# Retention and top-1 mixture of experts on one core: weight transfers moved behind GpSimd's scalings, their waits taken out

## The chip, the cores and the metric

The kernel runs on one core of one Trainium2 chip. The metric is the device time of one execution in microseconds (us), the median of several runs. The engines are named as in the profile: PE (TensorE, its weight loads apart as PEld), DVE (VectorE), ACT (ScalarE), POOL (GpSimd) and SP (SyncE, which here only issues DMAs).

## The reference

Eight heads of a decaying, causal linear attention over 8 sequences of 576 tokens, and behind it a top-1 mixture of 8 experts over all 4608 tokens. Cut to what matters:

```python
scores = (q @ k.T) / sqrt(64)                     # q, k, v: (8, 8, 576, 64)
D = where(i >= j, gamma[h] ** (i - j), 0)         # gamma = 1 - 2 ** (-5 - h)
x = ((scores * D) @ v), heads side by side        # (4608, 512)
logits = x @ w_gate                               # (4608, 8)
e = argmax(logits, axis=1)
gate = softmax(logits)[e]
out[token] = gate * (relu(x @ w1[e]) @ w2[e])     # w1: (8, 512, 1024), w2: (8, 1024, 512)
```

## The kernel before

The program has two phases. Phase 1 (the loop at L693) computes x, writes it as bf16 rows to the DRAM tensor x_rows, and routes the tokens of the first half. Phase 2 (L807 to L849) runs the experts: it gathers the rows of an expert, transposes them (trans), multiplies by w1 (mm1, PSUM tile pm), by w2 (mm2, PSUM tile py), and scatters the result.

Phase 1 goes over 40 blocks, i = 0 to 39: five for each sequence b, numbered c = 0 to 4. Blocks with c = 0 to 3 hold 128 tokens, the block with c = 4 the last 64. The five blocks of a sequence are called a batch here. The decay is split into a factor for each row of k and one for each row of q, so that k and q are scaled on POOL before PE sees them:

- scale_q(b, p) (L241) writes qq, one of two buffers; scale_k(i) (L250) writes kk, one of three. Both run on POOL. A block of the loop scales q for the next sequence, scale_q(b + 1, c), and k three blocks ahead, scale_k(i + 3).
- stage_TK(i + 2) transposes kk on PE into the PSUM tile psk, and ACT copies it to kT. stage_TQ(b + 1, c) transposes the qq that the same block has just scaled (psq). So PE wants qq in the block in which POOL makes it, and kk one block later.
- stage_R(i - 1) transposes the finished x back (psr) and writes it through SP's queue. For c = 4 its source is xTr. stage_L1 and stage_L2 make the logits (psl).
- stage_S(i + 1) updates the state from kk and v (pss); stage_AV(i) and stage_IN(i) add the two parts of the output in PSUM (psx), which DVE copies to xT; stage_SC(i + 1) makes the scores (pssc), which DVE multiplies by the mask into sc. `mark` keeps the last sc, kT, xT and se instruction.

The order on each engine is the order in which the program is written (a manual schedule). Around the change it is, in each block: scale_q, scale_k, load_k(i + 6), TK, TQ, L2, R, L1, S, AV, IN, SC, load_v(i + 6), then the weight transfers, then a step of the routing generator `rf` (L655, on DVE and PE, and one expert's two gathers xg on POOL per step once the slots are known).

The weights of experts 0 to 3 are fetched during phase 1 by load_w (L224), a DMA that POOL issues and that turns float32 in DRAM into bf16 in SBUF: 8 parts an expert, each 256 KB of bf16. Which block issues which part is a table (L688): one part each behind blocks 12, 16, 20, 24 and 28, three parts each behind blocks 33 to 39, and the last six behind the loop. Before, each of them waits: the first of a block for sc of block i + 1, the second for kT of block i + 2, the third for xT of block i:

```python
for (e, j), m in zip(early.get(i, ()), ("sc", "kT", "xT")):
    load_w(e, j, 4, wpool, mark.get(m))
```

POOL takes its instructions in order, so what stands behind a waiting transfer waits with it: scale_q and scale_k of the next block.

Of the kernel before, what the change touches and what calls it, by code (L numbers as in the profile page):

```python
# [41 lines left out]
def kernel(  # L42
# [22 lines left out]
    def after(ins, dep):  # L65

        if dep is not None:
            tc.add_manual_dep(ins.ins, dep.ins.name,
                              mybir.DependencyInfo(mybir.DependencyClass.Sync, mybir.DependencyReason.DATA),
                              reason="pace")  # L70
# [6 lines left out]
    wpool = ctx.enter_context(tc.tile_pool(name="wts", bufs=4))  # L77
# [20 lines left out]
    def load_q(b, g, dep=None, eng=None):  # L98

        if g == 0:  # L100
            qts[b] = ldq.tile([P, H, NCH, DH], F32, tag="q", name="qt")
        hs = slice(g * NP, (g + 1) * NP)
        after((eng or nc.sync).dma_start(out=qts[b][:, hs, :, :],
                                         in_=q[b, hs, 0:NCH * P, :].rearrange("h (p s) d -> p h s d", p=P)), dep)

    def load_kv(store, tag, src, i, dep):
        b, c = blocks[i]
        store[i] = ldk.tile([P, H, DH], F32, tag=tag, name=tag + "t")
        after(nc.sync.dma_start(out=store[i][:, :, :],
                                in_=src[b, :, c * P:(c + 1) * P, :].rearrange("h p d -> p h d")), dep)  # L110

    def load_k(i, dep=None):

        if i >= NB:
            return
        b, c = blocks[i]
        if c < NCH:
            load_kv(kts, "k", k, i, dep)
            return
        kts[i] = ldk.tile([P, H, DH], F32, tag="k", name="kt")  # L120
        for u in range(2):
            after(nc.sync.dma_start(out=kts[i][u * REM:(u + 1) * REM, :, :],
                                    in_=(q, k)[u][b, :, NCH * P:S, :].rearrange("h p d -> p h d")), dep)
# [100 lines left out]
    def load_w(e, part, n, pool, dep=None):  # L224

        if part == 0:
            wb[e] = (pool.tile([P, NPT, F], BF16, tag="w1", name="w1b"),
                     pool.tile([P, NFB, DM], BF16, tag="w2", name="w2b"))
        m = (NPT, NFB)[part // n] // n
        o = part % n * m  # L230
        w = (moe_w1, moe_w2)[part // n]
        after(nc.gpsimd.dma_start(out=wb[e][part // n][:, o:o + m, :],  # L232
                                  in_=w[e, o * P:(o + m) * P, :].rearrange("(c p) f -> p c f", p=P)), dep)
# [5 lines left out]
    mark = {}  # L239

    def scale_q(b, p):  # L241
        h0 = 2 * p
        qq = wkp.tile([P, NCH, P], F32, tag="qq")
        nc.gpsimd.tensor_tensor(  # L244
            out=qq[:, :, :].rearrange("p s (h d) -> p h s d", d=DH), in0=qts[b][:, h0:h0 + 2, :, :],
            in1=qg[:, 0:NCH, h0:h0 + 2].rearrange("p s h -> p h s").unsqueeze(3)
                .to_broadcast([P, 2, NCH, DH]), op=ALU.mult)
        qqs[(b, p)] = qq

    def scale_k(i):  # L250
        if i >= NB:
            return
        kk = wk3.tile([P, H, DH], F32, tag="kk")
        nc.gpsimd.tensor_tensor(out=kk[:, :, :], in0=kts.pop(i)[:, :, :],  # L254
                                in1=kg[:, blocks[i][1], :].unsqueeze(2).to_broadcast([P, H, DH]), op=ALU.mult)
        kks[i] = kk

    def stage_TQ(b, p):

        qq = qqs.pop((b, p))  # L260
        pst = psw.tile([P, 512], F32, tag="W", name="psq")
        for s_ in range(NCH):
            tr(pst[:, s_:512:NCH], qq[:, s_, :], ident[:, :])
        if b not in qTs:
            qTs[b] = wkp.tile([P, NP, 512], F32, tag="qT", name="qT")
        nc.scalar.copy(out=qTs[b][:, p, :], in_=pst[:, :])

    def stage_TK(i):
        if i >= NB:
            return  # L270
        kk = kks[i]
        pst = psw.tile([P, 512], F32, tag="W", name="psk")
        for p in range(NP):
            tr(pst[:, p * P:(p + 1) * P], kk[:, 2 * p:2 * p + 2, :].rearrange("p h d -> p (h d)"), ident[:, :])
        kT = wkp.tile([P, NP, P], F32, tag="kT")
        mark["kT"] = nc.scalar.copy(out=kT[:, :, :].rearrange("p a t -> p (a t)"), in_=pst[:, :])  # L276
        kTs[i] = kT
# [130 lines left out]
    def stage_L1(b):  # L408

        ps = psw.tile([P, 512], F32, tag="W", name="psl")  # L410
        xT, xTr = xTs.pop(b), xTs.pop((b, "r"))
        for a in range(NP):
            for c in range(NCH):
                mm(ps[32 * c:32 * c + 32, 0:P], wgp[:, 0, a, :], xT[:, c, a * P:(a + 1) * P], a == 0, a == NP - 1)
        for p in range(NP):
            o = (2 * (p % 2) + p // 2) * DH
            mm(ps[32 * p:32 * p + 32, P:P + DH], wgp[:, 1, p, :], xTr[:, o:o + DH], True, True)
        lt = wk1.tile([P, P + DH], F32, tag="lt")
        nc.vector.tensor_copy(out=lt[:, :], in_=ps[:, 0:P + DH])
        lts[b] = lt  # L420

    def stage_L2(b):
        lt = lts.pop(b)
        ps2 = psw.tile([P, 512], F32, tag="W", name="psl2")
        tr(ps2[:, 0:P], lt[:, 0:P], ident[:, :])
        tr(ps2[0:DH, P:2 * P], lt[:, P:P + DH], ident[:, :])
        t0 = b * NCOL
        nc.vector.tensor_copy(out=lg[:, t0:t0 + NCH, :],
                              in_=ps2[:, 0:P].rearrange("p (c n) -> p c n", n=32)[:, :, 0:E])
        nc.vector.tensor_reduce(out=lg[0:DH, t0 + NCH, :],  # L430
                                in_=ps2[0:DH, P:2 * P].rearrange("p (c n) -> p n c", n=32)[:, 0:E, :],
                                axis=AX.X, op=ALU.add)
# [18 lines left out]
    def make_routing():  # L451

        nc.gpsimd.memset(lg[:, :, :], 0.0)
        nc.gpsimd.memset(su1[:, :], -1.0)
        nc.gpsimd.affine_select(out=su1[:, :], in_=su1[:, :], pattern=[[-1, P]], base=0, channel_multiplier=1,
                                compare_op=ALU.is_ge, fill=0.0)
        nc.gpsimd.memset(onesb[:, :], 1.0)
        nc.gpsimd.tensor_copy(out=identb[:, :], in_=ident[:, :])
        nc.gpsimd.iota(iota_r[:, :], pattern=[[1, P]], base=0, channel_multiplier=0,
                       allow_small_or_imprecise_dtypes=True)  # L460
        nc.gpsimd.iota(rev[:, :], pattern=[[-1, E]], base=E, channel_multiplier=0,
                       allow_small_or_imprecise_dtypes=True)
        nc.gpsimd.memset(off[:, :], 0.0)
        nc.gpsimd.memset(off[REM:P, :].rearrange("p (b c) -> p b c", c=NCOL)[:, :, NCH:NCOL], 100.0)
        nc.gpsimd.memset(rst[:, :, :], 1.0)
        nc.gpsimd.memset(rst[:, :, 0:1], 0.0)
        nc.gpsimd.iota(hi[:, :], pattern=[[S // 64, B], [2, NCOL]], base=0, channel_multiplier=0,
                       allow_small_or_imprecise_dtypes=True)
        nc.gpsimd.iota(lo[:, :], pattern=[[1, 1]], base=1, channel_multiplier=1,
                       allow_small_or_imprecise_dtypes=True)  # L470
        nc.gpsimd.tensor_copy(out=fld[:, :, 0], in_=hi[:, :])
        nc.gpsimd.tensor_copy(out=fld[:, :, 1], in_=lo[:, :].to_broadcast([P, NT]))
# [215 lines left out]
    early = {12 + 4 * j: [(0, j)] for j in range(5)}  # L688
# [4 lines left out]
    for i, (b, c) in enumerate(blocks):  # L693
        if i == 1:
            make_routing()

        if c < NP and b + 1 < B:
            scale_q(b + 1, c)
        scale_k(i + 3)
        load_k(i + 6, mark.get("sc"))  # L700
        stage_TK(i + 2)
        if c < NP and b + 1 < B:
            stage_TQ(b + 1, c)
        if c == 1 and b > 0:
            stage_L2(b - 1)
        if i > 0:
            stage_R(i - 1)
        if c in (1, 3) and b + 2 < B:
            load_q(b + 2, c // 2, mark.get("kT"))
        if c == 0 and b > 0:  # L710
            stage_L1(b - 1)
        stage_S(i + 1)
        stage_AV(i)
        stage_IN(i)
        stage_SC(i + 1)
        load_v(i + 6, mark.get("xT"))
        for (e, j), m in zip(early.get(i, ()), ("sc", "kT", "xT")):
            load_w(e, j, 4, wpool, mark.get(m))
        if (b, c) == (B // 2, 1):
            rf = route_first()  # L720
        if rf is not None:
            steps(rf, 1.4)
# [232 lines left out]
```

## Time and profile before

| | us |
|---|---|
| median of 3 runs | 406.07 |
| lowest and highest run | 403.64, 408.64 |
| the profiled execution | 403.17 |
| its span, first to last instruction | 401.4 |

The profile shows one execution; its rows are times from the start of its span. Some 1.8 us lie outside the span. PE was busy for 338.4 us of it, POOL for 196.9, DVE for 161.1 and ACT for 127.4. The mean granted clock of TensorE was 0.95 of full speed.

### The profile page before, as it was taken

The numbers are of one execution on the slowest core, as the hardware profiler recorded it, in microseconds if no ns is written. First come the engines' busy times: TensorE is split into PE (matmuls) and PEld (weight loads), VectorE is DVE, ScalarE is ACT, GpSimd is POOL, SyncE is SP. The second block draws the span as 40 slices with busy tenths as digits, with TensorE's granted clock in tenths as the row PEclk, the third lists the DMA queues.
The fourth block names the chain that finished last, engine by engine and source line by source line (L and its number), as shares of the span: only waits on it lengthen the run. The fifth ranks groups of instructions, "written<-read, shape, count | busy, mean of one in ns | idle before, by whom it ended". The sixth has DMA issues, their size and how long they took to land.

```text
span 401.4 us, 11092 instructions
## 1 busy us (share of the span) xinstructions
PE 338.4 (84%) x4642; PEld 248.8 (62%) x4642; DVE 161.1 (40%) x358; ACT 127.4 (32%) x292; POOL 196.9 (49%) x241
## 2 busy tenths in 40 slices
PE   2599998889797969899668499989999999999950
PEld 2478787677676758678556367745555656566520
DVE  2043444315243627874165778323322322222220
ACT  2233434323331513423222022332233233342400
POOL 4784434161616153441875535785656555555120
PEclk9999999989998969999898679999999999999995
DMA  8969888766686766775999999989978332323120
GB/s 213 244 108 226 198 215 191 194 155 168 152 201 153 190 129 163 181 167 135 174 184 167 207 207 212 241 156 265 198 173 159 135 104 91 119 94 104 61 72 6
DMA packets 113084, 65.35 MB, mean 163 GB/s; under 512 B 83838, under 2 KB 105342, under 8 KB 113024
## 3 DMA queue, kind: packets, MB, share of 16 engines
q0 software_dynamic: 18176, 31.47, 35.9%
q1 hardware_dynamic: 93792, 32.02, 34.0%
q10 hardware_dynamic: 1056, 1.05, 0.9%
q8 instruction: 39, 0.64, 0.7%
q14 instruction: 21, 0.17, 0.1%
HBM read 67.14 MB, written 15.20 MB: 205 GB/s over the span
## 4 chain that ended last, share of the span: by engine, by line
PE 49%; issue 4%; DVE 3%; POOL 3%; DMA 1%; ACT 1%; SPq 0%; POOLq 0%; DVEq 0%; ACTq 0%
PE pm L60 18%; PE py L60 17%; PE psx L60 4%; PE pt L63 2%; PE pssc L60 2%; DMA x_rows<-xr 1%; PE psr L63 1%; POOL xg L637 1%; PE pss L60 1%; DVE xt L764 1%; PE psk L63 1%; PE psl L60 1%; PE pspl L60 1%; PE psq L63 1%; POOL kk L254 1%
## 5 line engine op out<-in xcount | busy, mean ns | idle before, releaser
L780 ACT ACTIVATE ht<-pm 128x384 bf16<-128x384 f32 (+1 forms) x96 | 50.6, 527 | 101.3 <-PE pm L60 100.8
L60 PE MATMUL pm<-xt,w1b 128*128 128x256 bf16 (+1 forms) x512 | 75.0, 307 | 2.4 <-DVE xt L764 2.4
L60 PE MATMUL py<-w2b,ht 128*128 128x512 bf16 x320 | 71.7, 379 | 0.0
L254 POOL TENSOR_TENSOR kk<-kt,kg 128x512 f32<-128x512 f32 x40 | 41.8, 1048 | 57.6 <-PE pss L60 25.3
L795 POOL DMA_INDIRECT out_dram<-ys,tids x40 | 40.9, 1022 | 59.4 <-DVE ys L794 52.7
L60 PEld LDWEIGHTS <-w1b 128*128 128x128 bf16 x512 | 51.3, 100 | 25.6 <-DVE xt L764 2.2
L60 PEld LDWEIGHTS <-ht 128*128 128x128 bf16 x320 | 30.8, 98 | 34.1
L794 DVE TENSOR_SCALAR ys<-py,gat 128x512 f32<-128x512 f32 x40 | 30.0, 750 | 47.5 <-PE py L60 44.9
L356 DVE COPY xT<-psx 128x512 f32<-128x512 f32 x32 | 22.1, 692 | 65.4 <-PE psx L60 65.4
L276 ACT COPY kT<-psk 128x512 f32<-128x512 f32 x40 | 23.8, 594 | 77.0 <-PE psk L63 50.5
L637 POOL DMA_INDIRECT xg<-x_rows,tidg x40 | 41.5, 1037 | 12.2 <-issue 7.9
L311 DVE TENSOR_TENSOR sc<-pssc,mask 128x1024 f32<-128x1024 f32 x32 | 39.1, 1222 | 19.6 <-issue 13.6
L63 PE MATMUL psk<-ident,kk 128*128 128x128 f32 x160 | 27.1, 293 | 18.2 <-POOL kk L254 18.2
L60 PE MATMUL psx<-sc,vt 128*64 128x128 f32 (+1 forms) x640 | 40.5, 278 | 0.8 <-DVE sc L311 0.8
L764 DVE COPY xt<-pt 128x512 bf16<-128x512 bf16 x40 | 15.5, 420 | 50.1 <-PE pt L63 47.3
L60 PE MATMUL pssc<-qT,kT 64*64 64x128 f32 (+1 forms) x1024 | 35.2, 257 | 0.0
L232 POOL DMA_DIRECT2D w1b<-in_moe_w_dram x24 | 15.4, 649 | 40.2 <-DVE sc L311 24.5
L244 POOL TENSOR_TENSOR qq<-qt,qg 128x512 f32<-128x512 f32 x32 | 33.9, 1061 | 1.8 <-DMA qt<-in_q_dram 1.4
L60 PEld LDWEIGHTS psx<-sc,vt 128*64 128x64 f32 (+1 forms) x640 | 32.7, 144 | 3.0 <-DVE sc L311 1.7
L63 PE MATMUL psq<-ident,qq 128*128 128x128 f32 x128 | 22.8, 309 | 13.6 <-POOL qq L244 13.6
L63 PEld LDWEIGHTS psk<-ident,kk 128*128 128x128 f32 x160 | 17.4, 144 | 24.1 <-POOL kk L254 20.0
L60 PEld LDWEIGHTS pssc<-qT,kT 64*64 64x64 f32 x1024 | 29.5, 137 | 1.8 <-issue 1.8
(118 smaller groups left out, 352.2 us busy)
## 6 DMA issues: line engine op xcount, KB each, us to landing
kt<-in_k_dram SPq DMA_DIRECT2D x32, 256.0 KB, 4.6
vt<-in_v_dram SPq DMA_DIRECT2D x32, 256.0 KB, 3.6
qt<-in_q_dram SPq DMA_DIRECT2D x14, 512.0 KB, 5.1
x_rows<-xr SPq DMA_DIRECT2D x32, 128.0 KB, 3.4
w1b<-in_moe_w_dram POOLq DMA_DIRECT2D x16, 256.0 KB, 6.3
w2b<-in_moe_w_dram POOLq DMA_DIRECT2D x16, 256.0 KB, 6.7
w1b<-in_moe_w_dram POOLq DMA_DIRECT2D x8, 512.0 KB, 7.2
w2b<-in_moe_w_dram POOLq DMA_DIRECT2D x8, 512.0 KB, 7.2
```

Source lines behind the costliest of these rows:

```text
L60: nc.tensor.matmul(out=out, lhsT=lhsT, rhs=rhs, start=start, stop=stop, skip_group_check=True)
L63: nc.tensor.transpose(out=out, in_=in_, identity=identity)
L244: nc.gpsimd.tensor_tensor(out=qq[:, :, :].rearrange("p s (h d) -> p h s d", d=DH), in0=qts[b][:, h0:h0 + 2, :, :], in1=qg[:, 0:NCH, h0:h0 ...
L254: nc.gpsimd.tensor_tensor(out=kk[:, :, :], in0=kts.pop(i)[:, :, :], in1=kg[:, blocks[i][1], :].unsqueeze(2).to_broadcast([P, H, DH]), op=A ...
L276: mark["kT"] = nc.scalar.copy(out=kT[:, :, :].rearrange("p a t -> p (a t)"), in_=pst[:, :])
L311: mark["sc"] = nc.vector.tensor_tensor(out=sc[:, :, :, :].rearrange("p j a i -> p j (a i)"), in0=pssc[:, :, :], in1=mask[:, :, :].rearrang ...
L356: mark["xT"] = nc.vector.tensor_copy(out=xTs[b][:, c, :].rearrange("p (w t) -> p w t", w=2), in_=psx[:, :, 0:2 * P])
L637: nc.gpsimd.indirect_dma_start(out=xg[:, :], out_offset=None, in_=x_rows[0:nr, :], in_offset=bass.IndirectOffsetOnAxis(ap=slots[ph][1][:, ...
L764: nc.vector.tensor_copy(out=xt[:, :, j * P:(j + 1) * P], in_=pt[:, :, :])
L780: nc.scalar.activation(out=ht[:, f0:f0 + per, :], in_=pm[:, :, :], func=AF.Relu)
L794: nc.vector.tensor_scalar(out=ys[:, :], in0=py[:, :], scalar1=gat[:, i:i + 1], scalar2=None, op0=ALU.mult)
L795: nc.gpsimd.indirect_dma_start(out=next(outs)[:, :], out_offset=bass.IndirectOffsetOnAxis(ap=tids[:, i:i + 1], axis=0), in_=ys[:, :], in_o ...
```

## The change

The weight transfers are issued right behind scale_k of their block, and they wait for no step of the block any more. The table of parts is the same.

```diff
@@ -697,6 +697,8 @@
         if c < NP and b + 1 < B:
             scale_q(b + 1, c)
         scale_k(i + 3)
+        for e, j in early.get(i, ()):
+            load_w(e, j, 4, wpool)
         load_k(i + 6, mark.get("sc"))
         stage_TK(i + 2)
         if c < NP and b + 1 < B:
@@ -714,8 +716,6 @@
         stage_IN(i)
         stage_SC(i + 1)
         load_v(i + 6, mark.get("xT"))
-        for (e, j), m in zip(early.get(i, ()), ("sc", "kT", "xT")):
-            load_w(e, j, 4, wpool, mark.get(m))
         if (b, c) == (B // 2, 1):
             rf = route_first()
         if rf is not None:
```

No engine's instructions change their order: between scale_k and the old place POOL has nothing else in a block. What changes is the waits. On POOL around block 12 (kk is the scaling of k for block 15, the row under w1b the scaling of q in block 13):

```order
 L254 TENSOR_TENSOR kk<-kt,kg 128x512 [waits DMAHW5_49,PE_49]
-L232 DMA w1b<-in_moe_w_dram 128x1024 [waits DVE_49]
+L232 DMA w1b<-in_moe_w_dram 128x1024
 L244 TENSOR_TENSOR qq<-qt,qg 128x2x4x64 [waits Pool_49]
 L254 TENSOR_TENSOR kk<-kt,kg 128x512 [waits DMAHW0_49,PE_49,Pool_49]
```

The transfer has lost its wait for DVE (sc of block 13); its place is the same. On POOL in blocks 33 and 34 (the first kk is that of block 36, the second that of block 37; xg are the gathers of expert 0, which need the slots tidg from DVE; DMASW0 to DMASW7 are eight completion counters that POOL's DMAs use in turn, each waiting for the one eight before it):

```order
 L254 TENSOR_TENSOR kk<-kt,kg 128x512 [waits DMAHW0_49,PE_49,Pool_49]
-L232 DMA w2b<-in_moe_w_dram 128x2x512 [waits DVE_49]
-L232 DMA w2b<-in_moe_w_dram 128x2x512 [waits Activation_49]
-L232 DMA w2b<-in_moe_w_dram 128x2x512
-L637 DMA xg<-x_rows,tidg_2892 128x512 [waits DMASW0_49]
+L232 DMA w2b<-in_moe_w_dram 128x2x512 x3
+L637 DMA xg<-x_rows,tidg_2892 128x512 [waits DMASW0_49,DVE_49]
 L637 DMA xg<-x_rows,tidg_2892 128x512 [waits DMASW1_49]
 L254 TENSOR_TENSOR kk<-kt,kg 128x512 [waits DMAHW4_49,PE_49]
```

Here the three transfers have lost their waits for DVE and ACT, and the first gather now names DVE itself. From block 34 on the transfers keep their wait for the counter of the eighth DMA before them.

## Rows read from the trace of the kernel before

**Rows 1.** The page, part 1: busy us (share of the span), instructions.

```profile
PE 338.4 (84%) x4642; PEld 248.8 (62%) x4642; DVE 161.1 (40%) x358; ACT 127.4 (32%) x292; POOL 196.9 (49%) x241
```

**Rows 2.** Who waited for whom: us in total, times, longest.

```profile
PE psq L63 <- POOL qq L244: 13.6, 6, 4.0
```

**Rows 3.** Timeline, PE, blocks 11 to 16: start, us, what, [idle before, releaser].

```profile
68.52 0.66 PE L63 MATMUL psk<-ident,kk 128*128 128x128 f32 x4
...
73.45 0.66 PE L63 MATMUL psk<-ident,kk 128*128 128x128 f32 x4
...
77.87 0.66 PE L63 MATMUL psk<-ident,kk 128*128 128x128 f32 x4
81.46 1.12 PE L63 MATMUL psq<-ident,qq 128*128 128x128 f32 x4 [2.94 <-POOL qq L244]
...
85.89 0.66 PE L63 MATMUL psk<-ident,kk 128*128 128x128 f32 x4
...
89.30 0.66 PE L63 MATMUL psk<-ident,kk 128*128 128x128 f32 x4
...
94.83 0.66 PE L63 MATMUL psk<-ident,kk 128*128 128x128 f32 x4
```

**Rows 4.** Timeline, POOL, the weight transfer of block 12; idle before and releaser.

```profile
79.55 0.76 POOL L232 DMA_DIRECT2D w1b<-in_moe_w_dram  x1 [7.24 <-DVE sc L311]
```

**Rows 5.** Timeline, PE, stage_R of c = 4, run in blocks 5, 10 and 30.

```profile
42.08 0.44 PE L63 MATMUL psr<-ident,xTr 128*128 128x128 f32 x2 [0.44 <-DVE xTr L379]
63.70 0.44 PE L63 MATMUL psr<-ident,xTr 128*128 128x128 f32 x2 [0.44 <-DVE xTr L379]
...
171.25 0.44 PE L63 MATMUL psr<-ident,xTr 128*128 128x128 f32 x2 [2.07 <-DVE xTr L379]
```

**Rows 6.** Timeline, PE, the first rows of blocks 34, 35 and 38.

```profile
188.62 0.66 PE L63 MATMUL psk<-ident,kk 128*128 128x128 f32 x4
...
195.92 0.66 PE L63 MATMUL psk<-ident,kk 128*128 128x128 f32 x4 [3.82 <-POOL kk L254]
...
215.15 0.66 PE L63 MATMUL psr<-ident,xT 128*128 128x128 f32 x4
```

**Rows 7.** Timeline, POOL, blocks 33 to 35: kk of blocks 36, 37 and 38.

```profile
180.98 1.04 POOL L254 TENSOR_TENSOR kk<-kt,kg 128x512 f32<-128x512 f32 x1 [0.92 <-POOL qq L244]
189.84 2.19 POOL L232 DMA_DIRECT2D w2b<-in_moe_w_dram  x3 [7.82 <-DVE sc L324]
...
194.81 1.05 POOL L254 TENSOR_TENSOR kk<-kt,kg 128x512 f32<-128x512 f32 x1
...
200.24 1.06 POOL L254 TENSOR_TENSOR kk<-kt,kg 128x512 f32<-128x512 f32 x1
```

**Rows 8.** Timeline, DVE: routing rows of block 29, and the slots of expert 0's gathers.

```profile
165.64 5.23 DVE L593 TENSOR_SCALAR rh<-iota_r,r 128x128 bf16<-128x128 bf16 x4
...
186.37 0.18 DVE L618 TENSOR_SCALAR tidg<-tid 128x16 int32<-128x16 f32 x1
```

**Rows 9.** The chain that ended last, in order of time: the last write of x_rows.

```profile
222.79 5.75 DMA x_rows<-xr
```

**Rows 10.** Timeline, DVE: the first copy of phase 2 and its wait.

```profile
228.66 0.76 DVE L764 COPY xt<-pt 128x512 bf16<-128x512 bf16 x2 [1.63 <-DMA x_rows<-xr]
```

**Rows 11.** Tile x_rows: landing of its transfers, all of them.

```profile
DMA to landing us min/median/max: 1.8/3.6/8.0
```

**Rows 12.** Busy us by window: PE, PEld, DVE, ACT, POOL, granted clock, DMA share, GB/s.

```profile
40.00:80.00 40.00, 36.89 (x772) 31.04 (x765) 16.89 (x24) 17.23 (x45) 14.23 (x15) 1.00 0.84 200
...
210.00:229.00 19.00, 12.08 (x226) 9.90 (x224) 11.53 (x38) 3.61 (x11) 11.78 (x18) 0.80 1.04 188
```

**Rows 13.** Timeline, POOL: transfers as phase 1 ends.

```profile
219.65 2.82 POOL L232 DMA_DIRECT2D w2b<-in_moe_w_dram  x4 [1.13 <-DVE sc L324]
...
229.52 0.70 POOL L232 DMA_DIRECT2D w2b<-in_moe_w_dram  x1 [0.69 <-DMA w2b<-in_moe_w_dram]
```

**Rows 14.** Tile kt: landing of its transfers, all of them.

```profile
DMA to landing us min/median/max: 2.9/4.4/8.1
```

## The prediction

> **What bounds the kernel now.** I read the busy times first, then the waits, then the timelines of PE and POOL in the stretches with weight transfers. PE is the busiest engine, 84% of the span, and POOL is half idle [rows 1]. So phase 1 should run at PE's speed unless something holds PE. In the list of waits PE's transposes of q wait 13.6 us in total for POOL's scaling [rows 2]. The timeline says when. The psk row marks the start of a block: blocks 11 and 12 take 4.93 and 4.42 us, block 14 takes 3.41 and block 15 5.53 [rows 3]. A whole undisturbed batch, blocks 5 to 10, takes 63.70 - 42.08 = 21.62 us [rows 5], which leaves 21.62 - 4.93 - 4.42 - 3.41 - 5.53 = 3.33 us for a block with c = 3. Block 13 has c = 3 and takes 8.02 us: PE waits 2.94 us for qq [rows 3]. The reader sees why on POOL: the transfer of block 12 waited 7.24 us for sc of block 13 [rows 4], and qq of block 13 stands behind it. [...]
>
> In block 33 it is the same with kk: kk of block 36 ends at 182.02, the three transfers start at 189.84, released by sc of block 34, and kk of block 37 follows at 194.81 [rows 7]. PE stands 3.82 us for it [rows 6].
>
> **The change, part by part.** No work is added or removed. At 26 transfers POOL no longer waits for DVE or ACT, and they keep their places in its order; what moves is the time at which POOL may go on.
>
> 1. *The five single transfers (blocks 12 to 28).* After the change the transfer of block 12 can start when kk before it ends, some 7 us earlier than 79.55, and qq of block 13 is done before PE asks for it, right behind the psk of 77.87 [rows 3]. From 63.70 to 171.25 four batches took 107.55 us, against 4 x 21.62 = 86.48 [rows 5]: an excess of 21.07 us. What of it stays? At 171.25 PE waits 2.07 us for xTr instead of the usual 0.44 [rows 5]; DVE stood in rows rh, four in 5.23 us [rows 8], while POOL caught up with the scalings that the transfer of block 28 had held back. Half of these 1.63 us I leave in, since some scalings will still fall there, and 0.6 us for the routing's matmuls and copies, which the undisturbed batch does not have (a choice; 0 and 2 are its bounds). 21.07 - 0.8 - 0.6 = 19.7 us won. The lower bound, if of each stall only the wait goes and the clock's part stays, is the 13.6 us of rows 2.
>
> 2. *Blocks 33 to 37.* From 188.62 to 215.15 PE needs 26.53 us for blocks 34 to 37 [rows 6]. Undisturbed they are 3.41, 5.53, 4.93 - 0.44 and 4.42 - 0.44 us, the 0.44 being four transposes of q that do not exist there (an estimate, two thirds of psk's 0.66, since neighbours overlap): 17.41. So 9.1 us are to be had, if kk comes in time. By POOL's order: the three transfers take 2.19 us [rows 7] and start at about 182.0; the two gathers wait for the slots, which DVE has at 186.6 [rows 8]; from the transfers' end to kk of block 37 the gathers took 194.81 - 192.03 = 2.8 us [rows 7]. So kk of block 37 starts at 189.4 and is there at 190.4; PE asks at 188.62 + 3.41 = 192.0. From one kk to the next, with three transfers and two gathers between, were 5.43 us [rows 7]: kk of block 38 is there at 195.9 (asked for at 197.6), that of block 39 at 201.3 (asked for at 202.1). The slack is 1.6, 1.7 and 0.8 us. I take the whole 9.1 us; zero is the lower bound.
>
> 3. *The end of phase 1.* The first expert's copies wait for the last x_rows write, which takes 5.75 us [rows 9] where the quickest takes 1.8 [rows 11]; the DMA engines are full there (share 1.04, [rows 12]). Will they still be? The transfers start 7.8 us earlier, but 27 of them at 1.4 us each (one of the last ones, 0.69 idle and 0.70 issuing, [rows 13]) are 38 us, and phase 1 ends 9 us earlier too. So the write meets the same crowd: 0 us. If the crowd were gone, the 1.63 us that DVE waited for it would be won and no more [rows 10]; if it were worse, 8.0 [rows 11] instead of 5.75 costs 2.3.
>
> 4. *The transfers' earlier place among k, v and q.* With PE undisturbed from 40 to 80 us the DMA share was 0.84 [rows 12]. One transfer in 21.6 us adds 1.4 us of full use, 0.065. That leaves about a tenth free; k takes 4.4 us to land, at most 8.1 [rows 14], and is wanted three blocks after its issue, 13 us. Cost 0. If the cover went, each of the four batches would be longer by up to the transfer's own 1.4 us: 0 to 5.6 in all.
>
> 5. *Phase 2.* Expert 0's eight parts land earlier than before. The last transfers stand at about the same place against the start of phase 2 as before (part 3), and they are expert 3's, which three others precede. 0.
>
> Sum: 19.7 + 9.1 = 28.8 us off the profiled execution's 403.17: 374.4. That execution is 2.9 us under the median of the runs, 406.07, and under the lowest of them; I put 2.1 us back and predict **376.5 us** as the median.
>
> [...] While POOL issued four transfers at 219.65 in 2.82 us [rows 13], 0.70 each, DVE was busy for 11.53 of the 19 us around [rows 12]; at 189.84, with DVE's sc behind them, three took 2.19, 0.73 each [rows 7]. But DVE's rh rows stood still beside POOL's scalings [rows 8]. [...]
>
> **Rivals.**
> [...]
> - *Only the waits go, the clock's part stays.* 13.6 instead of 19.7: 380.5, as a median 382.6. For: each gap need not vanish wholly. Against: in the 40 us up to the first transfer the granted clock was 1.00 [rows 12].
> - *Crowding, the slower side.* Without their waits the transfers compete with k and v. It decides once k lands later than 13 us after its issue. If each batch then were DMA-bound at 107.55 / 4 = 26.9 us, nothing is won in part 1, and in blocks 34 to 37 the nine transfers before kk of block 39 put 9 x 1.4 = 12.6 us ahead of the last k and v, with nothing won there either: 403.2 + 12.6 = 415.8. Against: 8.1 us is the longest landing of k [rows 14], and the last k is issued when only three transfers are ahead.
> - *It does nothing.* If other waits of the same rows (the counters, or POOL's own order) held the transfers as long, the time would be 406. For it speaks only that from block 34 on the counters stay.
>
> **How the numbers follow.** Forecast 0.72; lock or counters 0.11; clock's part stays 0.11; nothing 0.03; crowding 0.03. Low end: 374.4 less 1.6 for the last write and 1.4 for what part 1 left in, 371.4, so 371. High end: the two cases of partial gain are at 382.6 and 385.6, both together at 374.4 + 9.1 + 6.1 + 2.1 = 391.7; 389 leaves out the upper part of that and the last two cases. Faster by over 2% (what a measurement of this kernel can about tell from no change) 0.94, within 2% 0.03, slower 0.03.
>
> **What would show it.** Right: batches from block 10 to block 30 in 21.6 to 22 us each; no PE row of psq or psk waiting over 1 us for POOL after the start of the kernel; the granted clock at 0.97 or more from 80 to 190 us; POOL's weight rows released by nothing but its own order; blocks 34 to 37 in 17 to 18 us; the last x_rows write still over 4 us. Wrong: POOL's kk waiting for k's transfer in blocks 13 to 33, PE waiting for kk of blocks 38 or 39, DVE rows of sc or xT stretched beside POOL's DMA rows, or a start of phase 2 that waits for more than one write.

## The result, and the profile after

The changed kernel takes 383.09 us (median of 4 runs, 381.34 to 384.77), the kernel before beside it 407.36 us (median of 4, 403.64 to 409.62). The ratio is 0.9412, 95% interval 0.9324 to 0.9500: faster. The ratio and its interval are taken over runs in the faster of two states that the kernel before shows, so they need not be the quotient of two medians. The forecast was 376.5 us, range 371 to 389. The profiled execution took 381.34 us, its span is 379.6 us, its mean granted clock 0.963.

The stages, from the starts of the same rows in both traces (psr of xTr in blocks 10 and 30, psk of blocks 34 to 37, psr of block 38, DVE's first xt, the end of the span), in us:

| stage | before | after | won | reckoned |
|---|---|---|---|---|
| start to block 10 | 63.70 | 63.73 | 0.0 | 0 |
| blocks 10 to 29 | 107.55 | 87.05 | 20.5 | 19.7 (part 1) |
| blocks 30 to 33 | 17.37 | 17.37 | 0.0 | 0 |
| blocks 34 to 37 | 26.53 | 22.79 | 3.7 | 9.1 (part 2) |
| block 38 to the first xt | 13.51 | 13.30 | 0.2 | 0 (part 3) |
| phase 2, to the end of the span | 172.78 | 175.36 | -2.6 | 0 (part 5) |
| sum | 401.44 | 379.61 | 21.8 | 28.8 |

So the first part came as reckoned, and 7 us of the rest didn't come: 5.4 in blocks 34 to 37, 2.6 in phase 2.

The page of the changed kernel, part 1, which answers to [rows 1]: PE has the same 4642 matmuls and 6.6 us less busy time (fewer of them at the lower clock; the mean granted clock is 0.963 instead of 0.95), POOL the same 196.9 us.

```profile
PE 331.8 (87%) x4642; PEld 241.9 (64%) x4642; DVE 156.9 (41%) x358; ACT 127.1 (33%) x292; POOL 196.9 (52%) x241
```

Who waited for whom, after (us in total, times, longest), for [rows 2]: the 13.6 us for qq are 1.3. What is left of waits for kk are two at the start of the kernel (at 6.96 and 16.36 us).

```profile
PE psk L63 <- POOL kk L254: 11.3, 2, 7.0
...
PE psq L63 <- POOL qq L244: 1.3, 3, 0.7
```

POOL's timeline around the transfer of block 12, for [rows 4]: it starts when the kk before it ends, 8 us earlier than before, and qq of block 13 follows at 72.25.

```profile
70.48 1.04 POOL L254 TENSOR_TENSOR kk<-kt,kg 128x512 f32<-128x512 f32 x1 [2.37 <-PE pss L60]
71.47 0.76 POOL L232 DMA_DIRECT2D w1b<-in_moe_w_dram  x1
72.25 1.08 POOL L244 TENSOR_TENSOR qq<-qt,qg 128x512 f32<-128x512 f32 x1
```

PE's timeline, stage_R of c = 4 in blocks 10 and 30, for [rows 5]: four batches in 150.78 - 63.73 = 87.05 us, 21.76 each, and the wait for xTr at block 30 is down from 2.07 to 0.43.

```profile
63.73 0.44 PE L63 MATMUL psr<-ident,xTr 128*128 128x128 f32 x2 [0.44 <-DVE xTr L379]
...
150.78 0.44 PE L63 MATMUL psr<-ident,xTr 128*128 128x128 f32 x2 [0.43 <-DVE xTr L379]
```

PE's timeline, the first rows of blocks 34 to 38, for [rows 6]. The blocks take 5.90, 7.37, 4.77 and 4.75 us, where 3.41, 5.53, 4.49 and 3.98 were reckoned. The wait of 3.82 us for kk is gone, and no row names another one of that size.

```profile
168.16 0.70 PE L63 MATMUL psk<-ident,kk 128*128 128x128 f32 x4
...
174.05 0.85 PE L63 MATMUL psk<-ident,kk 128*128 128x128 f32 x4
...
181.43 0.66 PE L63 MATMUL psk<-ident,kk 128*128 128x128 f32 x4
...
186.20 0.49 PE L63 MATMUL psk<-ident,kk 128*128 128x128 f32 x3 [0.39 <-issue]
...
190.95 0.66 PE L63 MATMUL psr<-ident,xT 128*128 128x128 f32 x4
```

POOL's timeline beside them, for [rows 7]: kk of block 37 is done at 169.89 and PE takes it up at 174.05; that of block 38 at 175.33 for 181.43. Between two kk stand three weight transfers and two gathers xg.

```profile
168.84 1.05 POOL L254 TENSOR_TENSOR kk<-kt,kg 128x512 f32<-128x512 f32 x1
169.83 1.71 POOL L232 DMA_DIRECT2D w1b<-in_moe_w_dram  x3
171.84 1.06 POOL L637 DMA_INDIRECT xg<-x_rows,tidg  x1 [0.30 <-issue]
173.21 1.04 POOL L637 DMA_INDIRECT xg<-x_rows,tidg  x1 [0.30 <-issue]
174.27 1.06 POOL L254 TENSOR_TENSOR kk<-kt,kg 128x512 f32<-128x512 f32 x1
```

Where does PE's time go, then? The timeline of ACT and DVE in the same blocks shows it: copies of PE's results start late, released by something that the profile can't pair with a row of this core ("remote"), or by a PE row behind the one that they read. kT at 173.88 copies the psk of 168.16, which took 0.70 us: the copy comes 5 us late. The time is that of the gathers.

```profile
169.22 0.69 DVE L356 COPY xT<-psx 128x512 f32<-128x512 f32 x1 [2.78 <-PE pssc L60]
...
173.88 0.59 ACT L276 COPY kT<-psk 128x512 f32<-128x512 f32 x1 [6.66 <-remote]
```

Busy time by window, for [rows 12] (PE, PEld, DVE, ACT, POOL, granted clock, DMA share, GB/s). The granted clock is 1.00 in both windows; in the second PE is busy for 20.54 of 25 us and the DMA share is 1.12.

```profile
80.00:165.00 85.00, 82.34 (x1784) 69.83 (x1773) 48.66 (x100) 35.29 (x93) 39.81 (x41) 1.00 0.87 201
165.00:190.00 25.00, 20.54 (x410) 16.80 (x411) 9.42 (x24) 7.36 (x20) 20.50 (x25) 1.00 1.12 220
```

The last write of x_rows in the chain, for [rows 9], and DVE's first xt, for [rows 10]: 5.53 us instead of 5.75, a wait of 1.42 instead of 1.63.

```profile
198.59 5.53 DMA x_rows<-xr
```

```profile
204.25 0.76 DVE L764 COPY xt<-pt 128x512 bf16<-128x512 bf16 x2 [1.42 <-DMA x_rows<-xr]
```

Phase 2 has a pause of its own, which before doesn't have. POOL issues six gathers in a row from 227.16 and two scatters behind them (235.14 and 236.47); PE issues four matmuls py at 235.18, then stands from 236.2 to 237.8, ACT and DVE get its results late, and the granted clock is 0.50 from 239.2 to 242.6.

```profile
233.83 1.00 POOL L637 DMA_INDIRECT xg<-x_rows,tidg  x1 [0.30 <-issue]
...
235.18 1.03 PE L60 MATMUL py<-w2b,ht 128*128 128x512 bf16 x4
...
237.19 0.60 ACT L780 ACTIVATE ht<-pm 128x512 bf16<-128x512 f32 x1 [2.27 <-remote]
...
237.84 0.61 PE L60 MATMUL py<-w2b,ht 128*128 128x512 bf16 x2 [1.64 <-issue]
...
240.38 0.75 DVE L794 TENSOR_SCALAR ys<-py,gat 128x512 f32<-128x512 f32 x1 [7.74 <-PE py L60]
```

### The profile page after: what moved, and what is told of

Its sections match the earlier page's. It is cut to its first block, busy times and chain, and to the rows that moved or that the text cites. A ratio compares the mean times of both kernels' runs of the same rounds, so it can differ in the third digit from the quotient of the medians.

```text
span 379.6 us, 11084 instructions
## 1 busy us (share of the span) xinstructions
PE 331.8 (87%) x4642; PEld 241.9 (64%) x4642; DVE 156.9 (41%) x358; ACT 127.1 (33%) x292; POOL 196.9 (52%) x241
## 3 DMA queue, kind: packets, MB, share of 16 engines
q10 hardware_dynamic: 1056, 1.05, 0.9%
## 4 chain that ended last, share of the span: by engine, by line
PE 78%; DMA 4%; ACT 4%; DVE 4%; POOL 3%; issue 2%; another core or an unknown queue 1%; SPq 0%; ACTq 0%; POOLq 0%; DVEq 0%
PE pm L60 19%; PE py L60 18%; PE psx L60 12%; PE pssc L60 7%; PE psr L63 5%; PE psk L63 5%; PE pss L60 5%; PE psq L63 2%; PE pt L63 2%; PE psl L60 2%; DMA x_rows<-xr 1%; DMA kt<-in_k_dram 1%; DMA vt<-in_v_dram 1%; DVE xt L764 1%; ACT kT L276 1%
## 5 line engine op out<-in xcount | busy, mean ns | idle before, releaser
L60 PE MATMUL pm<-xt,w1b 128*128 128x256 bf16 (+1 forms) x512 | 74.0, 304 | 2.2 <-DVE xt L764 2.2
L60 PE MATMUL py<-w2b,ht 128*128 128x512 bf16 x320 | 73.6, 385 | 2.5 <-issue 1.6
L276 ACT COPY kT<-psk 128x512 f32<-128x512 f32 x40 | 23.8, 596 | 70.5 <-PE psk L63 41.8
L60 PE MATMUL psx<-sc,vt 128*64 128x128 f32 (+1 forms) x640 | 37.6, 266 | 1.0 <-DVE sc L311 1.0
L60 PE MATMUL pssc<-qT,kT 64*64 64x128 f32 (+1 forms) x1024 | 36.5, 255 | 1.2 <-issue 1.2
L60 PEld LDWEIGHTS psx<-sc,vt 128*64 128x64 f32 (+1 forms) x640 | 30.0, 136 | 3.2 <-DVE sc L311 2.2
L293 ACT COPY se<-pss 128x256 f32<-128x256 f32 x32 | 12.2, 380 | 36.8 <-PE psx L60 22.8
L60 PE MATMUL pss<-vt,kk 128*64 128x64 f32 x512 | 22.4, 231 | 0.0
```

The lines of the kernel that those rows point to most:

```text
L60: nc.tensor.matmul(out=out, lhsT=lhsT, rhs=rhs, start=start, stop=stop, skip_group_check=True)
```

## The experiments

Two questions were open: does the change's first part account for the gain, and what stops PE in blocks 34 to 37? Times are medians, ratios are to the kernel before run beside, which had medians of 408.37, 410.83, 410.88 and 407.28 us in the four rounds of experiments. "Blocks 34 to 37" and the stages are read as in the table above. A diff is against the changed kernel unless it says otherwise.

### First round: the two halves of the change, and fewer transfers

**again**: the changed kernel once more.

> The changed kernel once more. Blocks 34 to 37 took 22.8 us in its first profile instead of the 17.4 that were reckoned, with PE standing some 5.4 us behind no wait that the profile names. Theory A (PE stands because transfers and gathers fill the DMA engines there): blocks 34 to 37 take 21 to 24 us again, the pauses fall in the same blocks, the four batches before them take 87 us. Theory B (the pauses are chance of one execution): 17.5 to 19 us, or pauses elsewhere.

Measured 383.08 us (382.17 and 383.99), ratio 0.9396 (0.9298 to 0.9494). Blocks 34 to 37 take 22.21 us (6.22, 6.51, 4.71, 4.77), phase 2 176.46, with the clock falling at the same place. The pauses are not chance; theory B falls.

**singles**: only the five single transfers (blocks 12 to 28) at the new place, those from block 33 on at the old one with their old waits.

```diff
-        for e, j in early.get(i, ()):
+        for e, j in early.get(i, ()) if i < 33 else ():
             load_w(e, j, 4, wpool)
...
         load_v(i + 6, mark.get("xT"))
+        for (e, j), m in zip(early.get(i, ()) if i >= 33 else (), ("sc", "kT", "xT")):
+            load_w(e, j, 4, wpool, mark.get(m))
```

> The change for the five single transfers of blocks 12 to 28 alone; the three per block from block 33 on wait as before. Both theories: the four batches from block 10 to block 30 take 87 us instead of 107.6. Theory A: blocks 34 to 37 take 26 to 27 us with PE waiting for kk as before, no pauses without a named wait, and phase 2 is 2 to 3 us shorter than in the changed kernel: 382 to 385 us. Theory B: phase 2 as in the changed kernel: 385 to 388 us.

Measured 386.36 us (385.31 to 389.52), ratio 0.9497 (0.9407 to 0.9587). Blocks 10 to 29 take the same 87.05 us as in the changed kernel, blocks 34 to 37 28.11, over the 26 to 27 expected. Phase 2 takes 174.81, near the changed kernel's 175.36, and the time is theory B's: phase 2 is slow without the change from block 33 on as well. So part 1 of the prediction stands on its own, and by the medians the rest of the change is worth 386.4 - 383.1 = 3.3 us.

**tail**: the other half, the new place from block 33 on alone.

```diff
-        for e, j in early.get(i, ()):
+        for e, j in early.get(i, ()) if i >= 33 else ():
             load_w(e, j, 4, wpool)
...
         load_v(i + 6, mark.get("xT"))
+        for (e, j), m in zip(early.get(i, ()) if i < 33 else (), ("sc", "kT", "xT")):
+            load_w(e, j, 4, wpool, mark.get(m))
```

> The change for the transfers from block 33 on alone; the five single ones wait as before. The four batches take 107 to 108 us as before. Theory A: blocks 34 to 37 take 22 to 24 us with pauses, phase 2 is 2 to 3 us longer: 401 to 405 us, hardly faster than before. Theory B: blocks 34 to 37 take 17.5 to 19 us: 394 to 396 us.

Measured 403.57 us (399.0 to 404.6), ratio 0.9861 (0.9761 to 0.9961). Blocks 10 to 29 take 108.7 us, blocks 34 to 37 22.33: the pauses of the changed kernel are here too (6.19, 6.62, 4.30 and 5.21 us). The figures are those of theory A, which does not yet show its cause. The halves about add up: 5.0% and 1.4% (0.4% to 2.4%, so not clear of 2%) against 5.9% together.

**thin1**: one transfer a block in blocks 33 to 39, 20 behind the loop.

```diff
     for i in range(NB - 7, NB):
-        early[i] = [rest.pop(0) for _ in range(3)]
+        early[i] = [rest.pop(0)]
```

> The changed kernel with one transfer instead of three behind each of blocks 33 to 39 (the other fourteen follow behind the loop). Theory A: with a third of the transfers the DMA engines are not full, the pauses go, blocks 34 to 37 take 17.4 to 18.5 us and the time falls to 374 to 379 us. Theory B: 22 to 23 us for blocks 34 to 37 as in the changed kernel, 381 to 384 us.

Measured 376.81 us (375.73 to 379.47), ratio 0.9264 (0.9181 to 0.9346): faster than both kernels. Blocks 34 to 37 take 19.97 us: 5.87, 5.91, 4.20, 3.99. The last two are clean and block 35 nearly so; block 34 is 2.5 us too long, as in the changed kernel, though the transfers beside it are a third. The pause of phase 2 is gone (172.17 us). Theory A explains a part at best: what stayed lies at the first two pairs of gathers.

### Second round: gathers and transfers, each taken out

The expectations of this round and of the last one count phase 2 from 1.7 to 1.9 us ahead of the first xt; the measured figures here count from xt itself, as in the table.

**nogath**: the eight gathers of blocks 33 to 36 behind the loop, the transfers as in the changed kernel.

```diff
         for e in range(NA):
             yield None
-            gather(e, 0)
...
+    for e in range(NA):
+        gather(e, 0)
     for e, j in rest:
         load_w(e, j, 4, wpool)
```

> The changed kernel with the eight gathers xg of the first four experts issued behind the loop, ahead of the last six weight transfers, instead of two a block in blocks 33 to 36. The three weight transfers a block in blocks 33 to 39 stay. Theory G (PE stands while POOL's gathers move rows beside it): blocks 34 to 37 without their pauses, 17.4 to 18.5 us instead of 22.8, no PE row with over 0.6 us of lateness, and about 379 us as a median if phase 2 keeps its 177. Theory V (the bytes of three weight transfers a block, with k's and v's, leave no room): blocks 34 to 37 still over 21 us, 382 to 384 us. Theory C (PE's instructions come late, whatever POOL does): blocks 34 to 37 still 22 to 23 us, with the pauses at the same instructions.

Measured 383.47 us (382.36 to 384.89), ratio 0.9369 (0.9284 to 0.9454). PE's timeline, the first rows of blocks 34 to 38: 3.41, 5.85, 4.96 and 4.01 us, 18.2 together.

```profile
168.93 0.66 PE L63 MATMUL psk<-ident,kk 128*128 128x128 f32 x4
...
172.34 0.66 PE L63 MATMUL psk<-ident,kk 128*128 128x128 f32 x4
...
178.19 0.66 PE L63 MATMUL psk<-ident,kk 128*128 128x128 f32 x4
...
183.15 0.67 PE L63 MATMUL psk<-ident,kk 128*128 128x128 f32 x4
...
187.16 0.66 PE L63 MATMUL psr<-ident,xT 128*128 128x128 f32 x4
```

With three weight transfers a block left in and the gathers out, the pauses are gone: theory G, against V and C. The time as a whole wins nothing, against the 379 us expected: the eight gathers now run in a row from 192.59 to 203.34, and from block 38 to the first xt it takes 19.03 us instead of 13.30. DVE's copy of the logits there waits 6.52 us until 204.41. The price has moved, not gone.

**noearly**: no weight transfer in blocks 33 to 39, the gathers as in the changed kernel.

```diff
-    for i in range(NB - 7, NB):
-        early[i] = [rest.pop(0) for _ in range(3)]
```

> The changed kernel with no weight transfer in blocks 33 to 39: all 27 parts stand behind the loop. The gathers stay two a block in blocks 33 to 36. Theory G: the pauses stay, block 34 at 5.9 us and block 35 at over 5.9, blocks 34 to 37 together 19 to 22.8 us. Theory V: blocks 34 to 37 in 17.4 to 18.0 us. Theory C: 22 to 23 us as before the edit. The time as a whole: the parts of experts 0 to 3 start some 20 us later, so phase 2 may wait for expert 0's last parts or expert 1's; 375 to 385 us.

Measured 380.99 us (380.41 to 382.34), ratio 0.9314 (0.9232 to 0.9396). Blocks 34 to 37 take 5.49, 5.85, 5.93 and 4.00 us, 21.27 together: gathers alone, with no weight transfer beside them, make 21.27 - 17.41 = 3.9 of the 5.4 us. V falls.

**neither**: both edits.

> Both edits together: neither gathers nor weight transfers in blocks 33 to 39, all of them behind the loop. Theories G and V both expect blocks 34 to 37 at 17.4 to 18.0 us, the undisturbed figure. Theory C expects pauses still, over 21 us. The time as a whole 372 to 385 us, by what the late weights do to phase 2.

Measured 386.85 us (385.32 to 388.62), ratio 0.9466 (0.9379 to 0.9553). This was expected to be clean by G, and it isn't: block 36 takes 13.02 us. POOL, with nothing else to do, had reached the gathers early and ran all eight from 176.78 to 187.02, beside block 36. Two windows of this kernel (columns as above), ahead of the gathers and within them: in the second PE issues 8 matmuls in 2 us where it issued 66, with the DMA share at 0.53 and no weight transfer about.

```profile
174.00:176.00 2.00, 2.00 (x66) 1.91 (x57) 0.69 (x2) 0.54 (x2) 0.42 (x1) 1.00 0.11 25
...
184.00:186.00 2.00, 1.56 (x8) 0.62 (x8) 0.00 (x0) 0.00 (x0) 1.41 (x2) 0.50 0.53 129
```

Blocks 36 and 37 are 13.02 + 5.31 - 4.49 - 3.98 = 9.9 us too long, about the 10.2 us of the eight gathers. (The lower clock of the second window, granted 0.50, starts at 182.9, when PE has already faltered, so it didn't start the pause.) Nor does PE wait for instructions to be loaded: of the three packets of the instruction queues (q8, q14) from 174 to 192 us none lies between 178.7 and 190.0, and PE runs on at 188.37 without one.

**thin1_ng**: thin1 with the gathers behind the loop.

> The version with one weight transfer a block in blocks 33 to 39 (376.8 us), with the eight gathers issued behind the loop as well. Theory G: the two pauses that it still has (blocks 34 and 35 at 5.87 and 5.91 us instead of 3.41 and 5.53) go, some 2.5 to 2.9 us, so about 374 us. Theory V, by which one transfer a block is little enough: no change in blocks 34 to 37 (20 us), 376 to 378 us. Theory C: no change, 376 to 378.

Measured 387.28 us (386.46 to 389.34), ratio 0.9479 (0.9392 to 0.9566). Blocks 34 and 35 lost their pauses, as G expected (3.41 and 5.53 us), but POOL reached the eight gathers in block 36 and ran them from 180.48 to 190.72: block 36 takes 7.07 and block 37 11.85 us. The time was expected to fall and rose by 10. The misses of neither and thin1_ng suggest one thing: it matters how the gathers stand to one another.

### Third round: the price of a gather by itself

**extra**: gathers that nothing uses, put where PE is undisturbed. (It leaves nothing out; it adds work, so its time as a whole says nothing.)

```diff
+    xi = consts.tile([P, 1], I32, name="xi")
+    nc.gpsimd.iota(xi[:, :], pattern=[[1, 1]], base=0, channel_multiplier=1)
+    xw = moe_w2.rearrange("e f (h d) -> (e f h) d", h=2)
+    extra = {6: 2, 7: 2, 8: 2, 15: 1, 16: 1, 17: 1, 18: 1, 22: 4, 26: 2, 27: 2, 28: 2}
...
+        spare(extra.get(i, 0))
```

> The changed kernel with gathers added that nothing uses (128 rows of 1 KB of w2 into a buffer xs that lies free until the real gathers, fixed indices), at the end of blocks where PE is undisturbed: two each in blocks 6, 7 and 8 (the batch from block 5 to 10, which has no weight transfer), none in the batch from 10 to 15, one each in blocks 15 to 18, four in a row in block 22, two each in blocks 26, 27 and 28. It measures the price of a gather by itself; an undisturbed batch is 21.6 us. Theory G1, a fixed price for each gather (blocks 34 to 37 of the changed kernel less those without gathers, 22.79 - 18.22, over eight: 0.57 us): batches of 25.0, 21.6, 23.9, 23.9 and 25.0 us. Theory G2, the price comes from gathers close behind one another, singles are free: 21.6 with single gathers, over 24 with four in a row, 24 to 26 with three pairs. Theory L, the price belongs to the end of phase 1 alone (the gathers' source x_rows, which is still being written, or the routing's instructions beside): 21.6 to 22.2 in all five batches.

The one run took 401.55 us. PE's timeline, stage_R of c = 4, one row a batch, in blocks 5 to 30:

```profile
42.23 0.44 PE L63 MATMUL psr<-ident,xTr 128*128 128x128 f32 x2 [0.44 <-DVE xTr L379]
...
68.09 0.44 PE L63 MATMUL psr<-ident,xTr 128*128 128x128 f32 x2 [0.44 <-DVE xTr L379]
...
89.71 0.44 PE L63 MATMUL psr<-ident,xTr 128*128 128x128 f32 x2 [0.44 <-DVE xTr L379]
...
111.55 0.44 PE L63 MATMUL psr<-ident,xTr 128*128 128x128 f32 x2 [0.44 <-DVE xTr L379]
...
139.79 0.44 PE L63 MATMUL psr<-ident,xTr 128*128 128x128 f32 x2 [0.44 <-DVE xTr L379]
...
166.69 0.44 PE L63 MATMUL psr<-ident,xTr 128*128 128x128 f32 x2 [0.43 <-DVE xTr L379]
```

| batch | gathers added | us | over 21.62 |
|---|---|---|---|
| blocks 5 to 9 | three pairs | 25.86 | 4.24 |
| 10 to 14 | none | 21.62 | 0.00 |
| 15 to 19 | four single ones | 21.84 | 0.22 |
| 20 to 24 | four in a row | 28.24 | 6.62 |
| 25 to 29 | three pairs | 26.90 | 5.28 |

(The last batch has the routing's work as well; in the changed kernel it is 22.22 us.) That is theory G2: single gathers are almost free, pairs cost 1.4 to 1.6 us each on average, four in a row 6.6, of which some 3.4 are the lower clock from 125.0 to 131.8 (an estimate: half of 6.8; PE's psx<-sc, x16, took 1.97 us at 126.62 against 1.05 at 118.04, its pssc, x32, 1.93 at 129.43 against 1.05 at 119.50). A fixed price a gather (G1) would give 23.9 for the four single ones. L falls too: these gathers read w2, not x_rows, and stand far from the end of phase 1.

The timeline of POOL, PE and DVE beside the four in a row, which start at 119.50, 120.89, 122.20 and 123.51. PE's rows break up into groups of 5 or 6 with pauses between, put down to "issue"; the scores pssc, issued at 119.50 for 1.05 us, release DVE's sc only at 125.33, less than a microsecond behind the end of the last gather at 124.51.

```profile
122.83 0.62 PE L60 MATMUL pss<-vt,kk 128*64 128x64 f32 x6
123.51 1.00 POOL L696 DMA_INDIRECT xs<-in_moe_w_dram,xi  x1 [0.30 <-issue]
123.78 0.36 PE L60 MATMUL pss<-vt,kk 128*64 128x64 f32 x5 [0.34 <-issue]
...
125.25 0.51 PE L60 MATMUL pss<-vt,kk 128*64 128x64 f32 x5 [1.10 <-issue]
...
125.33 1.23 DVE L311 TENSOR_TENSOR sc<-pssc,mask 128x1024 f32<-128x1024 f32 x1 [4.54 <-remote]
```

**thin1_g1**: thin1 with one gather a block in blocks 33 to 39, the eighth behind the loop.

```diff
+    gat_on = []
...
             yield None
-            gather(e, 0)
+            gat_on.append(e)
...
             steps(rf, 1.4)
+        if gat_on:
+            n1 = len(gat_t)
+            gather(n1 // 2, 0, [n1 % 2])
+    while len(gat_t) < 2 * NA:
+        gather(len(gat_t) // 2, 0, [len(gat_t) % 2])
```

> The version with one weight transfer a block (376.8 us), with one gather a block in blocks 33 to 39 and the eighth behind the loop, instead of two a block in blocks 33 to 36. G1: the gathers that fall beside blocks 34 to 37 are about five instead of eight, and those of blocks 38 and 39 pay later: no change, 376 to 378 us. G2: blocks 34 and 35 lose their pauses of 2.5 us, about 374.5 us. L: pauses as before, 376 to 378 us.

Measured 375.40 us (375.12 to 376.63), ratio 0.9182 (0.9106 to 0.9258): the lowest median of all versions, though its runs overlap with those of thin1. PE's timeline, blocks 34 to 38:

```profile
168.91 0.66 PE L63 MATMUL psk<-ident,kk 128*128 128x128 f32 x4
...
172.84 0.66 PE L63 MATMUL psk<-ident,kk 128*128 128x128 f32 x4
...
178.33 0.66 PE L63 MATMUL psk<-ident,kk 128*128 128x128 f32 x4
182.53 0.66 PE L63 MATMUL psk<-ident,kk 128*128 128x128 f32 x4
...
188.03 0.66 PE L63 MATMUL psr<-ident,xT 128*128 128x128 f32 x4 [0.22 <-DVE xT L356]
```

Blocks 34 and 35 are down to 3.93 and 5.49 us, as G2 expected. The one block with a pause is 37, 5.50 instead of 3.98: there the seventh and the eighth gather stand close behind one another (184.36 and 185.72). Gathers need not be a whole block apart: the fourth to the seventh start 1.9 us from one another (178.57, 180.50, 182.44, 184.36), and block 36 beside them takes 4.20 us, as without gathers.

**thin1_hold**: thin1 with its last 20 transfers held until ACT has made the last xr (against thin1).

```diff
-    for e, j in rest:
-        load_w(e, j, 4, wpool)
     while steps(rf, 1.0):
         pass
     stage_R(NB - 1)
+    for n, (e, j) in enumerate(rest):
+        load_w(e, j, 4, wpool, mark["xr"] if n == 0 else None)
```

> The version with one weight transfer a block (376.8 us), with its last 20 weight transfers held until ScalarE has made the last rows xr, so that the last write of x_rows goes ahead of them. If that write is slow because of the weight transfers queued before it (5.73 us in the version as it was, and 1.60 us of it is what DVE's first xt waits for): it lands in 2 to 3 us, DVE's xt no longer waits for it, and the time is 375.2 us, unless phase 2 then waits for an expert's weights, which start some 7 us later. If the write is slow for another reason: it still takes over 5 us, and the time is 376 to 380 us.

Measured 387.10 us (385.94 to 388.38), ratio 0.9467 (0.9382 to 0.9551). The writes of the last block are as fast as the first case has it (1.7 and 1.8 us to land, against 5.1 and 5.7 in thin1), and DVE's first xt waits 0.29 us for a row of its own, lg, instead of 1.60 for the write; block 38 to xt is 12.09 us instead of 13.48. But phase 2 takes 182.99 us instead of 172.17. For weights PE waits only 0.36 us there (at 210.69); its long wait is for gathered rows. The six gathers of phase 2 start at 234.69, 9.4 us later than in thin1 (225.26), behind scatters and weight transfers that wait on POOL for earlier ones to land, and the first takes 11.38 us to land:

```profile
234.69 11.38 DMA xg<-x_rows,tidg
```

```profile
246.11 1.71 PE L63 MATMUL pt<-identb,xg 128*128 128x128 bf16 x12 [7.76 <-DMA xg<-x_rows,tidg]
```

So the crowd of transfers is what makes the last write slow, and holding the weights back costs more than it wins, though not by the wait for an expert's weights that was expected.

### Last round: phase 2

**split**: three of phase 2's six gathers in a row to be put behind the scatters.

```diff
             gather(0, 1)
-            if late:
-                gather(*late.pop())
...
             trans(*nxt)
+            if late:
+                gather(*late.pop())
```

> The changed kernel with phase 2's six gathers in a row (three of expert 0, three of expert 1, at 227 us) split: the three of expert 1 come behind the scatters of the expert in hand. PE's order is the same. In the changed kernel PE stands from 236.2 to 237.8 us and ScalarE and VectorE get its results up to 7.7 us late, right behind these six gathers and two scatters, and the clock falls for 3.4 us; phase 2 takes 177.05 us, in the kernel with one weight transfer a block, where another wait parted the six, 174.04. If the pause comes from gathers close behind one another: no pause there, phase 2 in 174 to 175 us, 380 to 381 us as a median. If it has another cause (PE's instructions or results late for a reason of their own): phase 2 in 176.5 to 178 us, 382 to 384 us.

Measured 384.67 us (384.26 to 385.93), ratio 0.9490 (0.9442 to 0.9539). The edit did nothing: the routing is ready one expert earlier than the edit supposes, so the six gathers are issued by another branch, and the trace has them in a row as before. It is one more run of the changed kernel (blocks 34 to 37 in 23.33 us, phase 2 in 177.98, the clock falling at the same place), and neither expectation was put to the test. The cause of phase 2's loss stays open.

## Why the prediction was right, and where it was off

**Part 1 was right.** 19.7 us reckoned, 20.5 measured, and by itself (singles) the same 87.05 us for four batches. The 0.8 us left in for rows rh were not needed: with POOL on time the wait for xTr at block 30 is 0.43 us. The 0.6 for the routing are there: blocks 25 to 29 take 22.22 us instead of 21.62. The clock came back whole, 1.00 from 80 to 190 us, where before it was 0.94 on average and 0.50 from 81.4 to 84.8, behind PE's gap in block 13. So the rival "the clock's part stays" falls.

**Part 2 named the right mechanism and mis-sized it:** "I take the whole 9.1 us" measured 3.7. The steps up to kk hold but for the last: kk of blocks 37, 38 and 39 were to be there 1.8, 7.3 and 12.7 us after the start of block 34, and were there after 1.7, 7.2 and 13.7. The third came 1.0 us later than reckoned, more than its slack of 0.8, but PE was late by then and waited for none of them. What failed is the step before, "So 9.1 us are to be had, if kk comes in time": it takes these blocks as undisturbed, 17.41 us, and leaves out the gathers, which the same part counts in POOL's order alone. Before, all eight start within blocks 34 to 37; after, six of them, and two in block 33. Why did the kernel before not show their price? The first and the third pair ran while PE waited for kk, which POOL makes behind them ([rows 6, 7], and 3.34 us before the psk of 209.55). The second and the fourth ran beside PE at work, at the lower clock (granted 0.50 from 197.4 to 200.8 and from 211.1 to 214.5), and PE's rows there have no pause. The rows of the second pair, before:

```profile
199.08 1.91 PE L60 MATMUL psx<-sc,vt 128*64 128x128 f32 x16
199.19 1.04 POOL L637 DMA_INDIRECT xg<-x_rows,tidg  x1 [0.30 <-issue]
...
200.92 1.09 PE L60 MATMUL pssc<-qT,kT 64*64 64x128 f32 x32
```

Whether the lower clock spared PE the pauses is not shown. nogath (18.22 us) shows that 17.41 was nearly right for the blocks without gathers; 22.79 - 18.22 = 4.6 of the missing 5.4 us are the gathers'.

**Parts 3 and 4 were right at 0.** The last write took 5.53 us, over 4 as foretold, and thin1_hold shows that it is the crowd of transfers. Crowding cost nothing in phase 1: three of the four batches with an early transfer took 21.61 us each, as undisturbed.

**Part 5 was wrong by 2.6 us:** "0" for phase 2. The argument, that the last transfers stand where they stood, looked at the weights alone. What stands there instead is a pause right behind six gathers in a row; that these are its cause is likely, but not shown. The stretch that holds these six, from the 65th matmul pm to the 129th, takes 23.1, 23.2 and 23.8 us in the three traces of the changed kernel and 21.5 to 23.8 in singles, tail, nogath, thin1_ng and extra, where the six are in a row as well; where another wait parts them (thin1, thin1_g1, neither, noearly) it takes 18.7 to 20.9, though in thin1 that wait is only 0.4 us long. In thin1_hold, where they are parted too, it takes 26.6, with the wait for their rows. And the kernel before has the six in a row, with PE at work beside them and 18.7 us for the stretch. Here its timeline, for that exception:

```profile
256.63 1.00 POOL L637 DMA_INDIRECT xg<-x_rows,tidg  x1 [0.30 <-issue]
257.11 3.66 PE L60 MATMUL pm<-xt,w1b 128*128 128x256 bf16 x32
```

So this is an agreement of most versions, not a proof, and the one run meant to test it missed. Against before, this stretch is 4.5 us longer in the changed kernel and the rest of phase 2 1.9 us shorter.

**The 2.1 us put back** for the profiled execution came to 383.09 - 381.34 = 1.75.

**The rivals.** The 385.6 us behind the chance "lock or counters" and in the high end was nearer to the 383.1 measured than the forecast. No run shows the term behind it, a lock or a counter at which each of POOL's DMAs between two kk stands for 1.2 us. In the changed kernel POOL's three transfers at 169.83 took 0.57 us each while DVE's xT and sc ran beside them, the two at 175.87 0.74 each beside an sc of 1.21 us, and POOL's first wait for an earlier transfer to land in blocks 33 to 39, 1.06 us, ends at 190.84, behind the last kk (done at 181.9). So kk came in time, and 4.6 of the missing 5.4 us are the gathers' (nogath). "Crowding" and "it does nothing" are excluded by the stages. The range held, and its upper part was there for a partial gain, though not for this cause.

**What stays open** is how a gather on POOL stops PE. The traces show that PE issues in groups with pauses for which no wait is named, and that its results reach ACT and DVE late, until the gathers end. They show too that pairs don't always cost: in the kernel before two pairs beside PE at the lower clock, in thin1 the pairs in blocks 35 and 36 cost 0.4 us and nothing, in extra the third pair (block 8) 0.1 us after two of 2.1 and 2.0. The DMA engines being full is not it (share 0.53 in neither), nor the loading of instructions (neither), nor the source or the indices (extra). Every timed run was recorded as well, so a part of the recording in it can't be excluded.

## What to carry to other kernels

A wait that goes is worth what the stage takes without it, and that has to be read from a stage with everything else in it: here the reckoning used blocks without gathers for blocks with them. When an engine has stood in a wait, look at what ran meanwhile; its price may have gone unseen there and comes due when the wait is gone. In a kernel like this one, space indirect transfers out (1.9 us apart was enough in thin1_g1) rather than two or four in a row, and load in such blocks only what must be there: both together gave 375.4 us against the change's 383.1. That holds for runs that are recorded; no run without recording is there to compare.

## What the runs showed of the hardware

- Gathers of 128 rows of 1 KB, 1.0 us of POOL each, beside phase 1's work on PE: four single ones, about a block apart, cost PE 0.2 us in all (extra); three pairs 4.2 us (extra); eight in a row 9.9 us (neither). PE begins to falter some 2 us after the first one starts (119.50 and 121.2 in extra, 176.78 and 179.2 in neither) and runs without such pauses from 1.4 to 2.7 us after the last has ended (188.37 after 187.02 in neither, 193.40 after 190.72 in thin1_ng).
- POOL's issue of one weight transfer took 0.53 to 0.84 us in the traces of before and after; after, three beside DVE's xT and sc took 0.57 each.
- The writes of phase 1's last block land in 5.1 to 5.8 us behind a crowd of transfers (before, after, thin1), in 1.7 to 1.8 ahead of them (thin1_hold).
